# S5 scan mixed with a SiLU FFN: less loaded at the head, two rows spread by TensorE, B's copies earlier, last tile in two halves

## The chip, the core and the metric

The kernel runs on one core of a Trainium2 chip. The time is device microseconds of one execution; several runs are made and their median is compared. Lower is better. TensorE is called PE below, VectorE DVE, ScalarE ACT, GpSimd POOL and SyncE SP, as the profile calls them.

## The reference

Input x is 2048 time steps of 448 features in bf16. Two branches are computed from the same x and mixed by a gate of one number per time step.

```
g = sigmoid((x * gate_w).sum(-1))
# branch A: a diagonal complex state space model, P = 448 states
Lam_bar = exp(dt * Lam);   dt = exp(log_dt)
Bu[t]   = B_bar @ x[t];    B_bar = ((Lam_bar - 1) / Lam)[:, None] * B
h[t]    = Lam_bar * h[t-1] + Bu[t]          # 2048 steps
a[t]    = 2 * real(C @ h[t]) + x[t] * Dskip
# branch B: an FFN, 448 -> 1792 -> 448
b       = silu(x @ w1) @ w2
out     = g * a + (1 - g) * b
```

## The kernel before, in words

Time steps are taken in pairs: `x2` has 1024 rows of two steps (an even and an odd one, 896 numbers). A tile is 128 such rows of one parity, so there are 16 tiles; tile `2 * kt + odd` is parity `odd` of row block `kt`.

All work is written out by hand as one list per engine. `T.op(engine, thunk, reads, writes)` appends an instruction to an engine's list and puts waits before it, worked out from the names of the buffers; each engine then works through its list in order. So an instruction that waits holds up everything behind it in its list. `T.dma` does the same for a transfer on the queue of SP or ACT. The 8 banks of PSUM are handed out in turn by `nxt`, so a matmul also waits for whoever has to empty the bank it is given.

**Head.** The even half of the first 512 rows of x2 is loaded in its natural layout (`XH`, here inside the buffer of `CO`), transposed by PE, and copied by DVE into `XT`. The other transposed parts of x come by transposing DMAs (`ldt`, L225), as B's do (`BT`). SP's queue goes through: half of `XH`, parts of W1, parameter rows, W1's second half (`W1Ed`), two of B's transposes, x odd half 0 (`XTo0`, `XTr0`), B's remainders (`BT2`, `BT3`), `XTe1`, `XTo1`, `XTr1`, then two rows spread over 128 partitions (`GWB` from gate_w, `DB` from Dskip), then natural x (`XN0`, `XN1`), later `W2` and C. ACT's queue has the other half of `XH`, two rows, and W1's last 64 rows twice: into partitions 0 to 63 (`W1Ea`) and 64 to 127 (`W1Ez`). The contraction is 448 = 3 * 128 + 64; two remainders of 64 rows run side by side in the halves of the PE array, so x's remainder is needed in both halves too: `swap_xr` (L237) copies it across with DVE.

The four parameter rows (log_dt, Lambda_re, Lambda_im, Dskip) lie in `R`; `mm_cols` turns them into columns with PE (bank 7), DVE and ACT work out the coefficients in a chain of 128x4 operations (`dt`, `ph`, ..., `f2`, `afr`, `sn`, `cs`, `rr`; L446 to L473). From `f2` POOL makes phases (`phases(pt)`, L484 and L486, two operations of 128x1024 for each of 4 blocks), DVE takes off the whole turns (`phases2`, L491), and ACT makes tables of sine and cosine (`tables`, L496 to L501). The two buffers `G0` and `G1` alternate between the phase blocks. DVE also makes two copies of B's remainder, into the other partition half (L523) and, packed, into `BR` (L525).

**Middle.** `ffn1(c)` computes one of four column blocks c of silu(W1 x) (matmuls L330, remainders L343; ACT empties the banks, L371). The first 7 feature blocks of block 0 go another way, `ffn1_first` (L360). `ffn2(c, q)` multiplies by W2 (L663). `bu(pt, h)` makes B x for state block pt (L701, remainders L713), ACT evicts it into `VE` and `HS` (L723, L725, L730). The recurrence of a state block is a generator on DVE (`scan`, and `scan3` for the last 64 states): the even step is folded into the odd one, the result turned by the tables, run through a real scan (L771), turned back. `gate` (L596) is x * gate_w, which ACT adds up (`gate2`, L613) and `gate3` makes factors of; `skip` (L604) is x * Dskip in place. Both work on four blocks of four tiles. `ffn2(0, q)` is evicted by DVE (L671) and adds the skip product. The generators are started piece by piece from one list near the end of the program (L918 to L1002), which so sets the order of every engine.

**Tail.** Per tile, C times the states is added to what ACT seeded into the bank (`yseed`, L868): five matmuls on state parts that come early (`YA`, `yopen`), two on the parts that come late (`YB`, `yclose`; L876). `yout` evicts with the gate, by ACT (L897, first eight tiles) or DVE (L900, last eight), and stores the tile.

Of the kernel before, what the change touches and what calls it, by code (L numbers as in the profile page):

```python
# [19 lines left out]
D = 448  # L20
# [126 lines left out]
def gated_mix(nc, A_x, A_Lambda_re, A_Lambda_im, A_B_re, A_B_im, A_C_re, A_C_im, A_log_dt,  # L147
              A_Dskip, B_x, B_w1, B_w2, gate_w, out):
    with ExitStack() as ctx:
# [36 lines left out]
        R = sb("R", [4, 512], BF16)  # L186
# [22 lines left out]
        def xg(b):  # L209
            if b < 2:  # L210
                return CO[:, 4 * b:4 * b + 4, :], [f"CO{m}" for m in (range(4) if b == 0 else (1, 4, 5, 6))]
            if b == 2:
                return OT[:, 0:4, :], [f"OT{i}" for i in range(4)]
            v = TMPS[:, :, :].rearrange("p a b -> p (a b)").bitcast(BF16)
            return v[:, 0:4 * D].rearrange("p (k c) -> p k c", k=4), [f"TMP{i}" for i in range(3)]
# [34 lines left out]
        XH = CO[:, :, :].rearrange("p a b -> p (a b)")[:, 0:2048].rearrange("p (k c) -> p k c", k=4)  # L250
        COK = [f"CO{m}" for m in range(7)]
        x0 = x2[0:512, 0:512].rearrange("(k p) c -> p k c", p=128)
        for i, eng in enumerate(("sp", "act")):
            T.dma(eng, lambda e, i=i: e.dma_start(XH[:, 2 * i:2 * i + 2, :], x0[:, 2 * i:2 * i + 2, :]),
                  writes=COK[i:i + 1])
# [9 lines left out]
        ld("sp", W1E[:, 0:3, FA:], B_w1[0:384, FA:].rearrange("(j p) f -> p j f", p=128), "W1Ed")  # L265
        ld("act", W1E[0:64, 3, :], B_w1[384:448, :], "W1Ea")
        T.op("act", lambda e: e.activation(JK[:, 0:1], HP[:, :], AF.Exp), reads=["HP"], writes=["JK0"])
        ld("act", W1E[64:128, 3, :], B_w1[384:448, :], "W1Ez")
# [10 lines left out]
        def load_xn(h):  # L279
            ld("sp", XN[:, 8 * h * D:8 * (h + 1) * D].rearrange("p (k c) -> p k c", k=4),  # L280
               x2[h * 512:(h + 1) * 512, :].rearrange("(k p) c -> p k c", p=128), f"XN{h}")
# [6 lines left out]
        for dst, src, key in ((GWB, gate_w, "GW"), (DB, A_Dskip, "DB")):  # L288
            ld("sp", dst[:, :], row(src).partition_broadcast(128).rearrange("p o n -> p (o n)"), key)
# [25 lines left out]
        def ffn1_mm(c, fbs):  # L315

            odd, h = c // 2, c % 2
            hs = slice(h * 512, (h + 1) * 512)
            x0 = 4 * odd
            banks = [nxt() for _ in fbs]  # L320
            xk = XO[h] + [f"XR{h}b"] if odd else XE[h] + [f"XR{h}a"]

            rf = half[0]

            def mains():
                for fb, bank in zip(fbs, banks):
                    def mm(pe, fb=fb, bank=bank):
                        ins = None
                        for j in range(3):
                            ins = pe.matmul(ps[:, bank, :], W1E[:, j, fb * 128:(fb + 1) * 128],  # L330
                                            XT[:, x0 + j, hs], start=(j == 0 and not rf), stop=(j == 2 and rf))
                        return ins
                    wk = ["W1Ej0", "W1Ej1", "W1Ej2"] if fb < NFA else ["W1Ed"]
                    T.op("pe", mm, reads=wk + xk, writes=[f"ps{bank}"])

            def rests():
                def rest(pe):
                    ins = None
                    for i, (fb, bank) in enumerate(zip(fbs, banks)):
                        up = (i % 2 == 1) != bool(odd)  # L340
                        p = slice(64, 128) if up else slice(0, 64)
                        x = XT[p, x0 + 3, hs] if up == bool(odd) else XR[p, hs]
                        ins = pe.matmul(ps[:, bank, :], W1E[p, 3, fb * 128:(fb + 1) * 128], x,  # L343
                                        start=rf, stop=not rf)
                    return ins
                T.op("pe", rest, reads=["W1Ea", "W1Ez"] + xk, writes=[f"ps{bank}" for bank in banks])
            for part in (rests, mains) if rf else (mains, rests):
                part()
            half[0] = not rf
            return list(zip(fbs, banks))  # L350

        def ffn1_first():

            banks = [nxt() for _ in range(NFA)]
            for j in range(4):
                for fb, bank in enumerate(banks):
                    up = j == 3 and fb % 2 == 1
                    p = slice(64, 128) if up else slice(0, 128 if j < 3 else 64)
                    x = XR[p, 0:512] if up else XT[p, j, 0:512]
                    T.op("pe", lambda pe, fb=fb, bank=bank, j=j, p=p, x=x: pe.matmul(  # L360
                        ps[:, bank, :], W1E[p, j, fb * 128:(fb + 1) * 128], x, start=(j == 0), stop=(j == 3)),
                        reads=[f"W1Ej{j}" if j < 3 else "W1Ez" if up else "W1Ea", "XR0a" if up else f"XTe0{j}"],
                        writes=[f"ps{bank}"])
                if j == 0:
                    yield
            nxt()
            yield list(enumerate(banks))
# [20 lines left out]
        def rd():  # L388
            T.op("dve", lambda e: e.tensor_copy(R[:, D:512], R[:, 384:448]), reads=["R0", "R1", "R2", "R3"],
                 writes=["Rd"])  # L390
# [17 lines left out]
        for j in range(4):  # L408
            for i in range(2):
# [5 lines left out]
                T.op("pe", mm, reads=[COK[i], "ID"], writes=[f"ps{3 + j}"])  # L415
        for j in range(4):
# [4 lines left out]
        next(first)  # L421
        T.op("pe", mm_cols, reads=["R0", "R1", "R2", "R3", "Rd", "ID"], writes=["ps7"])
        first = next(first)
        T.op("dve", lambda e: e.tensor_copy(
            PV[:, :, :], ps[:, 7, 0:32].rearrange("p (t c) -> p t c", c=8)[:, :, 0:4]),
            reads=["ps7"], writes=["PV"])

# [30 lines left out]
        pact("mag", col("ar"), AF.Exp, ["ar"])  # L458
        T.op("act", lambda e: e.activation(JK[:, 0:1], HP[:, :], AF.Silu), reads=["HP"], writes=["JK0"])
# [12 lines left out]
        pact("cs", col("afr"), AF.Sin, ["afr", "HP"], scale=-SIN_SCALE, bias=HP[:, 0:1])  # L472
        ptt("rr", col("mag"), col("mag"), ALU.mult, ["mag"])  # L473

# [32 lines left out]
        def tmp(m):  # L507
# [4 lines left out]
        phases(0)  # L512
        phases(3)
        phases2(0)
        phases2(3)
# [5 lines left out]
        phases(1)  # L521
# [5 lines left out]
            BT[:, :, :].rearrange("p j (c n) -> p j c n", c=2)[:, :, :, 384:448]), reads=BTK, writes=["BR"])  # L527
        phases2(1)
        phases2(2)
        swap_xr("dve", 1, 0)  # L530
# [61 lines left out]
        def gate():  # L592
            for b in range(4):
                v = XN[:, 4 * b * D:4 * (b + 1) * D].rearrange("p (k c) -> p k c", k=4)
                o, ks = xg(b)
                T.op("dve", lambda e, v=v, o=o: e.tensor_tensor(  # L596
                    o, v, GWB[:, :].unsqueeze(1).to_broadcast([128, 4, D]), ALU.mult),
                    reads=[f"XN{b // 2}", "GW", f"XD{b}"], writes=ks)
                yield

        def skip():
            for b in range(4):
                v = XN[:, 4 * b * D:4 * (b + 1) * D].rearrange("p (k c) -> p k c", k=4)
                T.op("dve", lambda e, v=v: e.tensor_tensor(  # L604
                    v, v, DB[:, :].unsqueeze(1).to_broadcast([128, 4, D]), ALU.mult),
                    reads=[f"XN{b // 2}", "DB"], writes=[f"XD{b}"])
                yield

        def gate2():
            for t in range(2 * NKT):  # L610
                o, ks = xg(t // 4)
                v = o[:, t % 4, :]
                T.op("act", lambda e, t=t, v=v: e.activation(v, v, AF.Copy, accum_out=Z[:, t:t + 1]),  # L613
                     reads=ks, writes=[f"Z{t}"])
                if t % 8 == 7:
                    s = t // 8
# [3 lines left out]
                if t % 4 == 3:  # L620
# [24 lines left out]
        def ffn2_seed(q, off):  # L645
# [3 lines left out]
                 reads=[f"XD{tile // 4}", "GRO"], writes=[f"ps{bank}"])  # L649

        def ffn2(c, q):
# [18 lines left out]
            if c == 0:  # L670
                T.op("dve", lambda e: e.scalar_tensor_tensor(  # L671
                    bs(tile), ps[:, bank, 0:D], GT[:, 3, tile:tile + 1], xd(tile), ALU.mult, ALU.add),
                    reads=[f"ps{bank}", "GRI", f"XD{tile // 4}"], writes=ks)
# [191 lines left out]
        def yseed(kt, odd):  # L865
# [3 lines left out]
                 reads=[f"BS{tile}" if kt < 4 else f"XD{tile // 4}"], writes=[f"ps{bank}"])  # L869
            seeds.append((kt, odd, bank))  # L870

        def yhalf(ms, kt, odd, bank):
            def mm(pe):
                ins = None
                for m in ms:
                    ins = pe.matmul(ps[:, bank, 0:D], state(kt, odd, m), CO[:, m, :], start=False, stop=(m == YB[-1]),  # L876
# [12 lines left out]
        def yout(tile, bank):  # L889
            kt, odd = tile // 2, tile % 2  # L890
            i = n_o[0] % 8
            n_o[0] += 1
            o = OT[:, i, :] if i < 4 else xg(3)[0][:, i - 4, :]
# [5 lines left out]
            else:  # L899
                T.op("dve", lambda e: e.scalar_tensor_tensor(  # L900
                    o, ps[:, bank, 0:D], g, bs(tile), ALU.mult, ALU.add),
                    reads=[f"ps{bank}", "GT1_1", f"BS{tile}"], writes=[f"OT{i}"] + extra)
            outs.append(T.dma("sp", lambda e: e.dma_start(
                out2[kt * 128:(kt + 1) * 128, odd * D:(odd + 1) * D], o),
                reads=[f"OT{i}"], writes=[f"out{tile}"]))
# [14 lines left out]
        g1, g2, g3 = gate(), gate2(), gate3()  # L920
        t0, t1, t2, t3 = [tables(pt) for pt in range(4)]
        s0, s3, s1, s2 = scan(0), scan3(), scan(1), scan(2, True)
        g0 = skip()
# [4 lines left out]
        run(t0)  # L928
# [3 lines left out]
        bu(3, 0)  # L932
        f = ffn1(1)
# [5 lines left out]
        run(g1, 2)  # L939
# [41 lines left out]
        tiles = [(kt, odd) for kt in range(4) for odd in (1, 0)]  # L981
# [15 lines left out]
        opened = [yopen(), yopen()]  # L997
        while opened:
            ahead()
            yout(*yclose(*opened.pop(0)))  # L1000
            if seeds:
                opened.append(yopen())  # L1002
        T.wait_all("sp", outs)
# [35 lines left out]
```

## Time and profile before

| what | value |
|---|---|
| median of 7 runs | 143.45 us (142.76 to 144.05) |
| the profiled execution | 144.22 us, span 142.5 us |
| granted PE clock | 1.00 |
| busy, PE / DVE / ACT / POOL | 134.8 / 120.2 / 94.7 / 30.6 us |
| moved by DMA | 12.53 MB, 16228 of 23215 packets under 512 B |
| XN<-in_A_x_dram, issue to landing | 10.7 us (median of two) |
| W<-in_B_w_dram (W2), issue to landing | 15.8 us |

The span is from the first instruction to the last. In a row of the timeline the columns are start, duration, engine, line, operation, output and input with shapes and count; in brackets the engine's idle time before it and what ended that. In a row of the chain of waits: start, duration, what. In a row of the waits: who waited for whom, total, times, longest. In a row of the stretches: from and to, length, then busy time with count for PE, PE's weight loads, DVE, ACT and POOL, then the granted clock, the share of the DMA engines and GB/s.

### The profile page before, as it was taken

What the parts mean: (1) busy time and instruction counts of PE and PEld (TensorE: products, weight loads), DVE (VectorE), ACT (ScalarE), POOL (GpSimd) and SP (SyncE); (2) the same over time, 40 slices, a digit from 0 to 9 for tenths busy, and PEclk for the clock granted to TensorE, in tenths of its full rate; (3) what the DMA queues carried; (4) which work ended last, traced back from release to release, by engine and by line L of the source; (5) the groups of instructions that cost most, each with busy time, mean ns of one, the idle gap of its engine ahead of it and who ended that gap; (6) DMA issues with size and microseconds to landing.
All of it is one profiled execution on the core that took longest, in us unless ns stands there. A gap on an engine that the chain in (4) does not pass through costs nothing.

```text
span 142.5 us, 1870 instructions
## 1 busy us (share of the span) xinstructions
PE 134.8 (95%) x692; PEld 61.3 (43%) x699; DVE 120.2 (84%) x148; ACT 94.7 (66%) x155; POOL 30.6 (21%) x36
## 2 busy tenths in 40 slices
PE   6999997999989997999999999999999999999991
PEld 2443333334335542443455434435555555555550
DVE  1573779807999999999999999999999999999543
ACT  1359899679999955995999473877412536889000
POOL 7139999500000000059960000000000000000000
DMA  4999797999689400030020000000000000221222
GB/s 126 301 273 221 143 187 141 141 396 381 170 142 124 93 1 0 0 74 0 9 69 0 0 0 0 5 0 0 0 0 0 0 5 1 95 97 64 69 92 97
DMA packets 23215, 12.53 MB, mean 88 GB/s; under 512 B 16228, under 2 KB 22632, under 8 KB 23208
## 3 DMA queue, kind: packets, MB, share of 16 engines
q1 hardware_dynamic: 22548, 11.34, 33.9%
q10 hardware_dynamic: 660, 1.08, 2.6%
q8 instruction: 5, 0.08, 0.2%
q14 instruction: 2, 0.02, 0.0%
HBM read 6.26 MB, written 1.84 MB: 57 GB/s over the span
## 4 chain that ended last, share of the span: by engine, by line
PE 59%; SPq 15%; DVE 15%; DMA 7%; issue 2%; DVEq 1%
PE ps L663 22%; PE ps L876 15%; SPq L225 13%; PE ps L330 13%; DMA XN<-in_A_x_dram 7%; PE ps L701 6%; DVE G L771 3%; DVE Q L734 3%; PE ps L343 2%; SPq L222 2%; DVE IOTA L671 2%; DVE CO L596 2%; DVE XN L604 1%; PE ps L713 1%; DVE HS L737 1%
## 5 line engine op out<-in xcount | busy, mean ns | idle before, releaser
L663 PE MATMUL ps<-W,AT 128*128 128x448 bf16 x224 | 42.9, 352 | 0.6 <-DMA W<-in_B_w_dram 0.6
L330 PE MATMUL ps<-XT,W1E 128*128 128x512 bf16 x143 | 32.9, 379 | 1.4 <-issue 1.3
L371 ACT ACTIVATE AT<-ps 128x1024 bf16<-128x1024 f32 (+1 forms) x32 | 27.3, 917 | 6.6 <-PE ps L343 6.3
L663 PEld LDWEIGHTS ps<-W,AT 128*128 128x128 bf16 x224 | 21.8, 98 | 21.5 <-ACT SIN L496 1.1
L330 PEld LDWEIGHTS ps<-XT,W1E 128*128 128x128 bf16 x147 | 13.6, 97 | 20.0 <-issue 4.7
L701 PE MATMUL ps<-XT,BT 128*128 128x512 bf16 x70 | 16.1, 379 | 0.1
L676 ACT ACTIVATE BT<-ps,GT 128x448 bf16<-128x448 f32 x8 | 5.1, 634 | 13.1 <-PE ps L663 13.1
L551 POOL TENSOR_TENSOR P<-P 128x4 f32<-128x4 f32 x5 | 4.5, 895 | 35.0 <-DVE P L558 34.7
L876 PE MATMUL ps<-CO,HS 128*128 128x448 bf16 x56 | 11.6, 352 | 0.0
L876 PE MATMUL ps<-CO,VE 128*128 128x448 bf16 x56 | 11.6, 352 | 0.0
L723 ACT ACTIVATE VE<-ps 128x1024 bf16<-128x1024 f32 (+1 forms) x8 | 7.3, 916 | 6.1 <-PE ps L713 5.3
L771 DVE TENSOR_TENSOR_SCAN G<-P,Q 128x1024 f32<-128x1024 f32 (+1 forms) x6 | 11.3, 1920 | 0.0
L701 PEld LDWEIGHTS ps<-XT,BT 128*128 128x128 bf16 x72 | 6.8, 98 | 9.0 <-issue 1.3
L737 DVE SCALAR_TENSOR_TENSOR HS<-VE,P,G 128x512 bf16<-128x512 bf16 (+1 forms) x10 | 8.1, 856 | 0.2
L725 ACT ACTIVATE HS<-ps 128x1024 bf16<-128x1024 f32 (+1 forms) x8 | 7.3, 916 | 0.8 <-PE ps L701 0.8
L876 PEld LDWEIGHTS ps<-CO,VE 128*128 128x128 bf16 x56 | 5.5, 98 | 5.1
L876 PEld LDWEIGHTS ps<-CO,HS 128*128 128x128 bf16 x56 | 5.5, 98 | 5.1
L737 DVE SCALAR_TENSOR_TENSOR G<-VE,P,HS 128x1024 f32<-128x1024 bf16 (+1 forms) x5 | 7.5, 1493 | 0.2
L734 DVE TENSOR_TENSOR Q<-G,COS 128x2048 bf16<-128x2048 f32 (+1 forms) x4 | 7.0, 1755 | 0.1
L734 DVE TENSOR_TENSOR Q<-G,SIN 128x2048 bf16<-128x2048 f32 (+1 forms) x4 | 7.0, 1750 | 0.0
L343 PE MATMUL ps<-XT,W1E 64*128 64x512 bf16 x25 | 6.8, 379 | 0.0
L596 DVE TENSOR_TENSOR CO<-XN,GWB 128x1792 bf16<-128x1792 bf16 x2 | 2.2, 1092 | 5.2 <-DMA XN<-in_A_x_dram 5.2
(118 smaller groups left out, 196.8 us busy)
## 6 DMA issues: line engine op xcount, KB each, us to landing
XN<-in_A_x_dram SPq DMA_DIRECT2D x2, 896.0 KB, 10.7
W<-in_B_w_dram SPq DMA_DIRECT2D x1, 1568.0 KB, 15.8
out_dram<-OT SPq DMA_DIRECT2D x8, 112.0 KB, 1.7
out_dram<-TMPS SPq DMA_DIRECT2D x8, 112.0 KB, 1.7
W1E<-in_B_w_dram ACTq DMA_DIRECT2D x3, 224.0 KB, 6.0
W1E<-in_B_w_dram SPq DMA_DIRECT2D x1, 672.0 KB, 8.4
HS<-HS SPq DMA_DIRECT2D x4, 128.0 KB, 2.3
W1E<-in_B_w_dram SPq DMA_DIRECT2D x2, 224.0 KB, 4.7
```

The lines of the kernel that those rows point to most:

```text
L225: return T.dma("sp", lambda e: e.dma_start_transpose(dst, src), reads=reads, writes=[key, *also], group=group)
L330: ins = pe.matmul(ps[:, bank, :], W1E[:, j, fb * 128:(fb + 1) * 128], XT[:, x0 + j, hs], start=(j == 0 and not rf), stop=(j == 2 and rf))
L343: ins = pe.matmul(ps[:, bank, :], W1E[p, 3, fb * 128:(fb + 1) * 128], x, start=rf, stop=not rf)
L371: T.op("act", lambda e: e.activation(a[:, fb:fb + n, :], ps[:, bank:bank + n, :], AF.Silu), reads=[f"ps{bank + i}" for i in range(n)], wri ...
L663: ins = pe.matmul(ps[:, bank, 0:D], a[:, fb, q * 128:(q + 1) * 128], W2[:, fb, :], start=(first and fb == 0), stop=(fb == NFB - 1), skip_g ...
L701: ins = pe.matmul(ps[:, bank, :], bt(slice(0, 128), j, m), XT[:, 4 * odd + j, hs], start=(j == 0 and not rf), stop=(j == 2 and rf))
L723: T.op("act", lambda e: e.activation(VE[:, m0:m0 + n, hs], ps[:, be[0]:be[0] + n, :], AF.Copy), reads=pe_, writes=[f"V{m}_{h}" for m in ms])
L725: T.op("act", lambda e: e.activation(HS[:, m0:m0 + n, 8 + h * 512:8 + (h + 1) * 512], ps[:, bo[0]:bo[0] + n, :], AF.Copy), reads=po_, writ ...
L734: T.op("dve", lambda e: e.tensor_tensor(o, a, b, op), reads=reads, writes=writes)
L737: T.op("dve", lambda e: e.scalar_tensor_tensor(o, a, s, b, ALU.mult, ALU.add), reads=reads, writes=writes)
L771: T.op("dve", lambda e, c=c, init=init: e.tensor_tensor_scan(G[:, c, w], rb, Q1[:, c, w], init, ALU.mult, ALU.add), reads=[f"Q1{c}", "rr", ...
L876: ins = pe.matmul(ps[:, bank, 0:D], state(kt, odd, m), CO[:, m, :], start=False, stop=(m == YB[-1]), skip_group_check=True)
```

## The change

W1's last 64 rows are loaded once, in two parts by column, and DVE copies each part into partitions 64 to 127 (`double`). W1's second half is loaded in two parts. The rows gate_w and Dskip are no longer spread by DMA: PE multiplies a one-hot column, repeated 128 times, with `R` (`spread`, bank 7), and DVE copies the result out (`spread_out`); gate_w is a fifth row of `R`. The natural x of the first load goes to its place in `XN`, and `load_xn(0)` brings only the columns that are missing; the blocks of `gate` and `skip` for the first 8 tiles go by parity accordingly. On DVE the first gate block and the copies of B come before `phases2(3)`, `phases(1)` and `phases(2)` change places, and `swap_xr` comes before the last two `phases2`. Cosine table 0 comes after `bu(3, 0)`. At the tail three tiles are opened instead of two, the first eight tiles have another order, and the last tile is computed, evicted and stored in two halves of 224 columns.

```diff
-        R = sb("R", [4, 512], BF16)
+        R = sb("R", [5, 512], BF16)
...
-        XH = CO[:, :, :].rearrange("p a b -> p (a b)")[:, 0:2048].rearrange("p (k c) -> p k c", k=4)
-        COK = [f"CO{m}" for m in range(7)]
+        FB = FA + 512
+        XH = XN[:, 0:8 * D].rearrange("p (k c) -> p k c", k=4)
+        XA = ["XA0", "XA1"]
...
-        ld("sp", W1E[:, 0:3, FA:], B_w1[0:384, FA:].rearrange("(j p) f -> p j f", p=128), "W1Ed")
-        ld("act", W1E[0:64, 3, :], B_w1[384:448, :], "W1Ea")
+        for key, f0, f1 in (("W1Ed", FA, FB), ("W1Ee", FB, F_FF)):
+            ld("sp", W1E[:, 0:3, f0:f1], B_w1[0:384, f0:f1].rearrange("(j p) f -> p j f", p=128), key)
+        ld("act", W1E[0:64, 3, 0:FA], B_w1[384:448, 0:FA], "W1Ea0")
         T.op("act", lambda e: e.activation(JK[:, 0:1], HP[:, :], AF.Exp), reads=["HP"], writes=["JK0"])
-        ld("act", W1E[64:128, 3, :], B_w1[384:448, :], "W1Ez")
+        ld("act", W1E[0:64, 3, FA:], B_w1[384:448, FA:], "W1Ea1")
+        ld("act", R[4:5, 0:D], row(gate_w), "R4")
...
         def load_xn(h):
+            c0 = 0 if h else 512
...
-        for dst, src, key in ((GWB, gate_w, "GW"), (DB, A_Dskip, "DB")):
-            ld("sp", dst[:, :], row(src).partition_broadcast(128).rearrange("p o n -> p (o n)"), key)
         load_xn(0)
         load_xn(1)
...
+        def spread(i, c0):
+            T.op("pe", lambda pe: pe.matmul(ps[:, 7, c0:c0 + D], ID[0:i + 1, i:i + 1].to_broadcast([i + 1, 128]),
+                                            R[0:i + 1, 0:D], start=True, stop=True),
+                 reads=["R0", "R1", "R2", "R3", "ID"] + (["R4"] if i == 4 else []), writes=["ps7"])
+
         T.op("pe", mm_cols, reads=["R0", "R1", "R2", "R3", "Rd", "ID"], writes=["ps7"])
-        first = next(first)
+        spread(3, 64)
+        next(first)
...
+        def spread_out(dst, c0, key):
+            T.op("dve", lambda e: e.tensor_copy(dst[:, :], ps[:, 7, c0:c0 + D]), reads=["ps7"], writes=[key])
+
+        def double(i):
+            f = slice(i * FA, (i + 1) * FA)
+            T.op("dve", lambda e: e.tensor_copy(W1E[64:128, 3, f], W1E[0:64, 3, f]), reads=[f"W1Ea{i}"],
+                 writes=[f"W1Ez{i}"])
...
         pact("mag", col("ar"), AF.Exp, ["ar"])
+        spread_out(DB, 64, "DB")
+        spread(4, 0)
...
         pact("cs", col("afr"), AF.Sin, ["afr", "HP"], scale=-SIN_SCALE, bias=HP[:, 0:1])
+        double(0)
+        first = next(first)
         ptt("rr", col("mag"), col("mag"), ALU.mult, ["mag"])
+        spread_out(GWB, 0, "GW")
+        double(1)
...
-        phases(0)
-        phases(3)
-        phases2(0)
-        phases2(3)
         ptt("lr", col("mag"), col("cs"), ALU.mult, ["mag", "cs"])
...
-        phases(1)
+        phases(0)
+        phases(3)
+        phases2(0)
+        next(g1)
         phases(2)
         T.op("dve", lambda e: e.tensor_copy(BT[0:64, 3, :], BT[64:128, 3, :]), reads=BTK[2:4],
              writes=["BTz"] + BTK[2:4])
...
+        phases2(3)
+        phases(1)
+        swap_xr("dve", 1, 0)
+        phases2(2)
         phases2(1)
-        phases2(2)
-        swap_xr("dve", 1, 0)
...
-        run(t0)
+        run(t0, 2)
         bu(0, 0)
         load_w2()
         load_c()
         bu(3, 0)
+        run(t0)
...
-        run(g1, 2)
+        run(g1, 1)
         run(g0, 2)
...
-        tiles = [(kt, odd) for kt in range(4) for odd in (1, 0)]
+        tiles = [(0, 1), (1, 1), (0, 0), (2, 1), (1, 0), (3, 1), (2, 0), (3, 0)]
...
-        opened = [yopen(), yopen()]
+        opened = [yopen(), yopen(), yopen()]
+        kt, odd = tiles[-1]
         while opened:
             ahead()
             yout(*yclose(*opened.pop(0)))
-            if seeds:
+            if len(seeds) > 1 or tiles:
                 opened.append(yopen())
+        yseed(kt, odd)
+        for c in (slice(0, D // 2), slice(D // 2, D)):
+            kt, odd, bank = seeds.pop(0)
+            yhalf(YA + YB, kt, odd, bank, c)
+            yout(2 * kt + odd, bank, c)
```

## The prediction

> **What bounds the kernel now.** I read four views in this order: the page's busy row, the table of stretches (who is idle when), the chain of waits, then the timeline of the head and the tail.
>
> ```profile
> PE 134.8 (95%) x692; PEld 61.3 (43%) x699; DVE 120.2 (84%) x148; ACT 94.7 (66%) x155; POOL 30.6 (21%) x36
> ```
> ```profile
> 20.00:21.00 1.00, 0.77 (x6) 0.11 (x4) 0.93 (x2) 0.97 (x2) 0.92 (x2) 1.00 1.28 281
> 22.00:23.00 1.00, 0.78 (x3) 0.20 (x2) 1.00 (x2) 1.00 (x2) 0.92 (x2) 1.00 1.18 264
> 23.00:24.00 1.00, 0.33 (x2) 0.22 (x3) 0.83 (x3) 1.00 (x3) 0.76 (x3) 1.00 0.36 80
> 39.00:40.00 1.00, 0.57 (x3) 0.08 (x1) 1.00 (x3) 0.97 (x2) 0.00 (x0) 1.00 0.46 81
> 54.00:55.00 1.00, 0.24 (x4) 0.11 (x4) 1.00 (x3) 0.88 (x1) 0.00 (x0) 1.00 0.00 0
> 55.00:139.40 84.40, 84.00 (x437) 39.96 (x436) 79.82 (x81) 52.36 (x75) 11.15 (x9) 1.00 0.08 25
> ```
> The number after the length of a stretch is TensorE's (PE's) busy time. From 55 us to its last matmul PE is busy 84.00 of 84.40 us at granted clock 1.00, so that part only moves as a block. Whatever the change can give lies in PE's holes before 55 us: 1.17 us in 20 to 24 (0.23 + 0.05 + 0.22 + 0.67; the 0.05 is in 21:22), 0.62 us in 39 to 41, 0.76 us in 54 to 55. Together 2.55 us, 1.8% of the span.
>
> ```profile
> 23.28 9.79 DMA XN<-in_A_x_dram
> 33.06 0.02 issue
> 33.09 1.10 DVE CO L596
> ...
> 52.46 2.33 DVE IOTA L671 x4
> 54.79 0.05 issue
> 54.84 0.60 PE ps L713 x4
> ```
> ```profile
> DVE CO L596 <- DMA XN<-in_A_x_dram: 5.2, 1, 5.2
> PE ps L663 <- DMA W<-in_B_w_dram: 0.6, 1, 0.6
> ```
> The chain names the last hole: VectorE (DVE) stands idle 5.2 us for the natural x, then works without a pause to L671, which frees the banks PE needs at 54.84. The second wait is the hole at 40: W2, issued at 24.30, lands 15.8 us later. The holes of 20 to 24 are waits for DVE: L713 for the BR copy until 20.99, and the second FFN1 column block for `swap_xr`, which ends at 23.57 while PE starts at 23.67.
>
> ```profile
> 9.64 1.04 DVE L449 TENSOR_TENSOR P<-P 128x4 f32<-128x4 f32 x2
> 9.44 1.16 POOL L484 TENSOR_SCALAR FP<-IOTA,P 128x1024 f32<-128x1024 f32 x1 [5.25 <-DVE P L449]
> 19.32 0.62 DVE L523 COPY BT<-BT 64x896 bf16<-64x896 bf16 x1 [0.83 <-DMA BT<-in_A_B_im_dram]
> 139.03 1.27 DVE L900 SCALAR_TENSOR_TENSOR TMPS<-ps,GT,SIN 128x448 bf16<-128x448 f32 x2 [0.64 <-PE ps L876]
> ```
> The first two rows show a 128x4 operation that takes 0.16 us elsewhere held until GpSimd's (POOL's) instruction is over at 10.60. The last is the tail: two evictions of 0.68 us end at 140.30, 0.94 us after the last matmul (139.36).
>
> **The change, part by part.** The profiled execution took 144.22 us, span 142.5 and 1.72 around it; it is 0.77 above the median of 143.45. I make the sum on the span and subtract it from the median.
>
> *Transfers.* Gone: W1's second remainder (224 KB), GWB and DB (112 KB each), half of the first x block (512 KB); 960 KB. SP loses two issues (0.58 + 0.42 + 0.1 between them = 1.1 us) and gains one (W1Ee, about 0.43), which falls before the BT issue that sits 5.17 us in the queue anyway, so it costs nothing; without that cover it would be 0.43 us on every transpose. ACT's queue loses one W1 issue's bytes, and gains R4 (0.24 us) at 4 us, before its first wait at 4.7. 224 KB at some 300 GB/s bring the transposes 0.75 us forward, BT's landing from about 19.3 to 18.5; XN0 and W2 are issued 0.75 + 1.1 = 1.85 us earlier. In 28 to 36 us the engines move 380 to 410 GB/s, so 512 KB less before W2 are 1.3 us more. Estimate for W2: 37 to 38.8 instead of 40.1. XN0 (384 KB, first after the transposes) about 28.
>
> *VectorE's added work.* Two broadcast rows from PSUM (`spread_out`), between 0.42 (64x512 bf16 from PSUM, L418) and 0.68 each (128x448 f32 from PSUM, L671); I take 0.6. Two copies `double`: the nearest row is L523, same shape, 0.62 us, of which 0.38 overlap POOL's instruction that ends at 19.70; bare 0.24. The ends are 0.24 and 0.24 + 1.1 (one POOL instruction). The first `spread_out` lies in the serial chain ph to f2: POOL begins at about 10.05, not 9.44, and ACT's cosine comes at 11.3.
> Here a rule speaks against the change. The Trainium skill, "SBUF — State Buffer", section "Who interferes with whom", says that GpSimd and a VectorE copy in a two-port mode, or a VectorE operation with two SBUF inputs, hold a shared port pair exclusively, and the later one waits for the whole instruction. The rows above agree (0.62 for 0.24; 1.04 for two times 0.16). By the bare rows the four additions cost 1.7 us of VectorE; by the rule up to one POOL instruction (1.05 to 1.16) more at `double(0)`, `double(1)`, the gate product and the B copies. In the trace a second ready DVE instruction slips in before POOL's next one (`rr` directly after `afr`, 10.5 to 10.68), so I let `double(0)` run right behind `afr`: 11.3 to 11.55. PE's odd remainders waited for W1Ez until 11.11 and now wait until 11.55: **+0.45 us**, or +1.5 if the port is lost there. The two added matmuls on PE (0.2 each) vanish in that wait; alone they would be 0.4.
>
> *VectorE's order.* `double(1)`, lr, li, lis each can meet a POOL instruction; I put `phases2(0)` at 16.2 to 17.4 (before: 11.76). That is hidden: ACT reaches its sine table only at 18.43. Gate block 0 (1.09, L596) to 18.5, the B copies behind BT's landing and one POOL instruction to about 20, `phases2(3)` (1.22) to 21.2, `swap_xr` (0.29) to 21.5, 22.5 with another port loss. Behind it `phases2(2)` and, waiting for POOL's last operation, `phases2(1)` to about 26; the scan's first step starts there instead of 23.70, 2.4 us late. COS0 moves behind bu(3,0)'s evictions on ACT, whose 1.20 us wait at 25.8 takes it.
> PE: bu(0,0) and its remainder to 21.3 without a wait, bu(3,0) to 22.8, second FFN1 block from 22.8, not 23.67. So the 1.17 us are recovered and 0.3 to 0.45 given back at 11.5: **net -0.85**.
>
> *Middle.* PE reaches FFN2 at 39.58 - 0.85 = 38.7, with W2 there: **-0.62**. DVE from 26.1: scan step and scan3's step (4.2), gate 1 at about 30.4 (XN0 landed), skip 0 and 1 (2.1), 33.5; steps of 2.7 and 1.5, two gates (2.1), `turn` (8.2), gate3 (1.0) and three L671 (1.8) give 51 to 51.7 for the fourth, which was over at 54.79. PE wants the banks at 54.06 - 1.5 = 52.6: no hole, **-0.76**. That has about 1 us to spare. ACT, solid from 34 to 51.7, moves with PE at 31 (-0.85) and loses its 0.23 wait for CO, so the bank it frees last is there at 50.65, when PE wants it at 50.8; late next is therefore ACT, by 0 to 0.2 us.
>
> *Tail.* Fourteen half-width matmuls instead of seven: their weight loads take 0.098, a half of 448 columns takes about 0.094, so 1.45 us against 1.31, +0.14. Behind them DVE does three evictions of 0.68 and two of about 0.44; the last ends 0.73 after PE instead of 0.94: **-0.07**. A rule against it: the Trainium skill, "DMA: Bandwidth & Descriptors", "Specifications", has DMA line rate from 512 B and a read-modify-write below; the halves write 448 B rows. By the row (112 KB land in 1.7 us) a half is no slower and the sum stays at -0.07; if the rule costs the halved write what halving saves and another 0.3, +0.2. I take the row.
>
> Sum: -0.85 - 0.62 - 0.76 - 0.07 = -2.3; less 0.1 for ACT, **-2.2 us**: span 140.3, median **141.2 us**.
>
> **Rivals.**
> 1. *The port eats the head.* Every added copy loses against POOL: first remainders at 12.6 (+1.5), `swap_xr` at 23 to 23.6. Then 20 to 24 gives nothing; W2 and L671 still give 1.4: 142.1. For it: the two rows above. Against: POOL has only eight such operations and two of them must wait for VectorE.
> 2. *W2 does not come sooner.* Its end lies in 37 to 40, where only 80 to 90 GB/s flow; if what holds its last packets is not what was removed, PE waits until 40.1 again, and with it falls everything before. Left are L671's 0.76 and the tail, with ACT taking some: 142.7 to 143.4, say 143.0, no change to speak of. Against: 512 KB are missing from the full-rate stretch.
> 3. *Slower: VectorE is queued behind B.* The B copies now stand ahead of `phases2(3)`, `swap_xr`, the last phases and the scan. If BT lands at T, `swap_xr` ends between T + 2.0 (0.3 + 0.2 + 1.2 + 0.3) and T + 4.1 (two port losses). It decides when the FFN1 block starts past 23.67 + 0.62 + 0.76 + 0.07 + 0.72 = 25.8, that is T beyond about 22.8. At T = 23.5, block at 26.5: 143.45 + 2.83 - 1.45 = 144.8. For it: BT's issues are held 2.95 and 5.17 us, the queue is congested. Against: BT landed by 19.3 with more bytes ahead.
>
> **How the numbers follow.** About 0.5% (0.7 us) is what a measurement of this kernel tells from no change. Main case 0.60 (141.2; its own range 140.2 to 142.2), rival 1 0.15 (142.1), rival 2 0.12 (143.0), rival 3 and other losses 0.13 (144.8). Faster: 0.60 + 0.15 = 0.75; same 0.12; slower 0.13. The range runs from 139.9 (all holes, 2.55 us; 0.3 at the tail; 0.7 for scatter, as the lowest single run lies 0.7 below the median) to 143.8, past rival 2's end by the same scatter on its upper side; rival 3 is left out.
>
> **What would show it.** Right: no DVE wait on XN of several us; PE idle in 20 to 24 under 0.4; FFN2 starting below 39; no L713 wait on L671; `double(0)` just behind `afr`. Wrong: `double(0)` over 1 us, or PE's first remainders after 12; W2 landing at 40; a new PE wait for `swap_xr` or ACT's L371; a hole in PE after 55 where VectorE's last scan is late.

## The result, and the profile after

| what | before | after |
|---|---|---|
| median of all runs shown | 143.45 us (31 runs, 142.67 to 144.37) | 141.74 us (12 runs, 141.39 to 142.78) |
| the profiled execution, and its span | 144.22 us, 142.5 us | 141.74 us, 140.0 us |
| granted PE clock | 1.00 | 1.00 |
| W2, issue to landing | 15.8 us | 10.5 us |
| moved by DMA | 12.53 MB | 11.54 MB |

The ratio after to before is 0.989, with a 95% interval of 0.9868 to 0.9912: the interval lies clear of 1, so it is faster, by 1.7 us in the medians. The two profiled executions lie 2.5 us apart; the difference between 1.7 and 2.5 is taken up below. Against the prediction of 141.2 us the kernel is 0.5 us slower, inside the range.

The page of after, its busy row, and then the first row of its part on the chain that ended last (shares of the span by engine):

```profile
PE 134.9 (96%) x701; PEld 62.8 (45%) x708; DVE 124.8 (89%) x153; ACT 94.8 (68%) x156; POOL 30.0 (21%) x36
...
PE 92%; DVE 4%; issue 1%; DVEq 0%; ACT 0%
```

PE works as long as before (134.8 us then), DVE 4.6 us longer, and the chain now is PE almost from end to end. The stretches of after (PE's busy time stands behind the length):

```profile
11.00:12.00 1.00, 0.65 (x4) 0.21 (x5) 0.94 (x3) 0.59 (x2) 0.92 (x2) 1.00 1.28 287
12.00:13.00 1.00, 0.84 (x7) 0.31 (x5) 1.00 (x2) 0.92 (x3) 0.83 (x2) 1.00 0.92 175
20.00:21.00 1.00, 1.00 (x7) 0.34 (x7) 1.00 (x2) 0.97 (x2) 0.63 (x1) 1.00 0.89 121
22.00:23.00 1.00, 0.95 (x6) 0.42 (x5) 0.97 (x2) 1.00 (x2) 0.94 (x1) 1.00 1.09 213
23.00:24.00 1.00, 1.00 (x6) 0.46 (x5) 1.00 (x1) 1.00 (x3) 0.92 (x2) 1.00 0.59 124
39.00:40.00 1.00, 1.00 (x7) 0.49 (x5) 1.00 (x2) 0.97 (x2) 0.00 (x0) 1.00 0.11 22
54.00:55.00 1.00, 1.00 (x6) 0.49 (x5) 0.97 (x2) 1.00 (x2) 0.00 (x0) 1.00 0.00 0
55.00:137.20 82.20, 81.80 (x433) 39.67 (x433) 76.16 (x78) 51.50 (x74) 11.27 (x9) 1.00 0.08 25
```

All three holes are closed: in 20 to 24, at 39 and at 54 PE is busy, up to 0.05 us. Of PE's idle time behind 10 us and ahead of the block from 55 on, what is left stands in 11 to 13 (0.35 + 0.16 us); the 0.35 are a wait for the copy of W1's last remainder rows. The timeline of after, DVE's rows of that place, and POOL's first two operations:

```profile
10.41 0.96 DVE L464 TENSOR_TENSOR P<-P 128x4 f32<-128x4 f32 x1
11.41 0.39 DVE L440 COPY W1E<-W1E 64x896 bf16<-64x896 bf16 x1
11.82 0.89 DVE L464 TENSOR_TENSOR P<-P 128x4 f32<-128x4 f32 x1
```
```profile
10.21 1.16 POOL L505 TENSOR_SCALAR FP<-IOTA,P 128x1024 f32<-128x1024 f32 x1 [6.02 <-DVE P L464]
11.45 1.26 POOL L507 TENSOR_SCALAR G<-FP 128x1024 f32<-128x1024 f32 x1
```

`afr` at 10.41, a 0.16 us operation, is held until POOL's operation is over at 11.37. `double(0)` (L440) starts just before POOL's next one and takes 0.39 us, and the operation behind it is held again, to 12.71. PE takes the odd remainders up at 11.85.

The chain of after in the middle, and the last evictions from its timeline:

```profile
38.87 5.30 PE ps L697 x28
44.20 5.47 PE ps L697 x28
49.72 2.54 PE ps L735 x11
52.26 0.97 PE ps L747 x8
```
```profile
136.30 1.39 DVE L934 SCALAR_TENSOR_TENSOR TMPS<-ps,GT,SIN 128x448 bf16<-128x448 f32 x3
```

L697 (L663 before), L735 (L701) and L747 (L713) follow each other without a wait for W2 or for DVE. The last eviction ends at 137.69, 0.53 us after PE's last matmul at 137.16; before it was 0.94.

### The profile page after: what moved, and what is told of

It is laid out like the page before. It is cut to its first block, busy times and chain, and to the rows that moved or that the text cites. A ratio compares the mean times of both kernels' runs of the same rounds, so it can differ in the third digit from the quotient of the medians.

```text
span 140.0 us, 1895 instructions
## 1 busy us (share of the span) xinstructions
PE 134.9 (96%) x701; PEld 62.8 (45%) x708; DVE 124.8 (89%) x153; ACT 94.8 (68%) x156; POOL 30.0 (21%) x36
## 2 busy tenths in 40 slices
DMA packets 23473, 11.54 MB, mean 82 GB/s; under 512 B 16485, under 2 KB 23018, under 8 KB 23466
## 4 chain that ended last, share of the span: by engine, by line
PE 92%; DVE 4%; issue 1%; DVEq 0%; ACT 0%
PE ps L697 30%; PE ps L331 23%; PE ps L910 14%; PE ps L735 13%; PE ps L344 4%; PE ps L747 2%; PE ps L403 2%; PE ps L361 2%; DVE P L464 1%; PE ps L414 1%; DVE TMPS L934 1%; DVE P L461 1%; DVE DB L436 0%; DVE W1E L440 0%; DVEq L1046 0%
## 5 line engine op out<-in xcount | busy, mean ns | idle before, releaser
L697 PE MATMUL ps<-W,AT 128*128 128x448 bf16 x224 | 43.0, 353 | 0.0
L697 PEld LDWEIGHTS ps<-W,AT 128*128 128x128 bf16 x224 | 21.8, 98 | 20.9 <-ACT AT L372 0.5
L372 ACT ACTIVATE AT<-ps 128x1024 bf16<-128x1024 f32 (+1 forms) x32 | 27.3, 916 | 5.5 <-PE ps L344 5.1
L735 PE MATMUL ps<-XT,BT 128*128 128x512 bf16 x70 | 16.1, 380 | 0.1
L600 POOL TENSOR_TENSOR P<-P 128x4 f32<-128x4 f32 x5 | 5.6, 1121 | 28.2 <-DVE P L607 27.9
L910 PE MATMUL ps<-CO,VE 128*128 128x448 bf16 (+1 forms) x63 | 11.6, 332 | 0.0
L910 PE MATMUL ps<-CO,HS 128*128 128x448 bf16 x56 | 11.6, 353 | 0.0
L805 DVE TENSOR_TENSOR_SCAN G<-P,Q 128x1024 f32<-128x1024 f32 (+1 forms) x6 | 11.3, 1918 | 0.0
L735 PEld LDWEIGHTS ps<-XT,BT 128*128 128x128 bf16 x72 | 6.8, 97 | 9.0 <-issue 1.3
L910 PEld LDWEIGHTS ps<-CO,VE 128*128 128x128 bf16 x63 | 6.1, 98 | 4.7
L910 PEld LDWEIGHTS ps<-CO,HS 128*128 128x128 bf16 x56 | 5.5, 98 | 5.1
L934 DVE SCALAR_TENSOR_TENSOR OT<-ps,GT,BT 128x448 bf16<-128x448 f32 x4 | 2.7, 684 | 4.4 <-PE ps L910 4.4
## 6 DMA issues: line engine op xcount, KB each, us to landing
W<-in_B_w_dram SPq DMA_DIRECT2D x1, 1568.0 KB, 10.5
```

The source lines that it names most:

```text
L372: T.op("act", lambda e: e.activation(a[:, fb:fb + n, :], ps[:, bank:bank + n, :], AF.Silu), reads=[f"ps{bank + i}" for i in range(n)], wri ...
L600: T.op("pool", lambda e: e.tensor_tensor(col(o), a, b, op), reads=ra, writes=[o])
L697: ins = pe.matmul(ps[:, bank, 0:D], a[:, fb, q * 128:(q + 1) * 128], W2[:, fb, :], start=(first and fb == 0), stop=(fb == NFB - 1), skip_g ...
L735: ins = pe.matmul(ps[:, bank, :], bt(slice(0, 128), j, m), XT[:, 4 * odd + j, hs], start=(j == 0 and not rf), stop=(j == 2 and rf))
L805: T.op("dve", lambda e, c=c, init=init: e.tensor_tensor_scan(G[:, c, w], rb, Q1[:, c, w], init, ALU.mult, ALU.add), reads=[f"Q1{c}", "rr", ...
L910: ins = pe.matmul(ps[:, bank, c], state(kt, odd, m), CO[:, m, c], start=False, stop=(m == YB[-1]), skip_group_check=True)
```

## The experiments

All ratios are to the kernel before, run beside it on the same chip. Diffs are against the kernel before where the label begins with b, against the one after where it begins with a.

**b_again: the kernel before, unchanged, profiled once more.** No edit.

> The kernel before, unchanged, profiled once more. The profiled pair moved by 2.5 us, the medians by 1.7. Theory: the profile of before was one of its slow executions, with a larger hole in PE behind W2 or behind VectorE's wait for x than a usual one has; then this profile has a span of 141.4 to 142.0 and its holes before 55 us add up to about 1.8 us, not 2.55. Rival: the holes are the same in every execution and the extra time lies elsewhere (outside the span or after 55 us); then the holes are again 2.5 us.

It took 143.19 us, span 141.5, and lies 0.3 us below the median of 143.45; the first profile (144.22) lies 0.8 above. Its row of the waits, then two rows of its timeline, where the odd remainders begin and where the third hole was:

```profile
DVE CO L596 <- DMA XN<-in_A_x_dram: 3.1, 1, 3.1
```
```profile
11.53 0.39 PE L360 MATMUL ps<-XR,W1E 64*128 64x512 bf16 x1 [0.46 <-DMA W1E<-in_B_w_dram]
...
53.40 1.04 PE L713 MATMUL ps<-XT,BT 64*128 64x512 bf16 x8
```

DVE waits 3.1 us for the natural x and not 5.2, because XN lands 9.8 us after its issue and not 10.7, and the eight L713 matmuls run in one piece. The hole of 0.76 us does not exist in this execution, and the wait for W2 is 0.4 us, not 0.6. So the third term of the sum belongs to the execution that was profiled first. The odd remainders of the first block wait for their load until 11.53, where the first profile had 11.11. PE's idle time in 20 to 24 is there in both (0.24 and 0.79 us in 22 to 24 here).

**b_tail: the tail alone, on the kernel before.**

```diff
-        def yhalf(ms, kt, odd, bank):
+        def yhalf(ms, kt, odd, bank, c=slice(0, D)):
...
-        tiles = [(kt, odd) for kt in range(4) for odd in (1, 0)]
+        tiles = [(0, 1), (1, 1), (0, 0), (2, 1), (1, 0), (3, 1), (2, 0), (3, 0)]
...
-        opened = [yopen(), yopen()]
+        opened = [yopen(), yopen(), yopen()]
...
+        for c in (slice(0, D // 2), slice(D // 2, D)):
+            yhalf(YA + YB, kt, odd, bank, c)
+            yout(2 * kt + odd, bank, c)
```

> Before with the tail alone changed (order of the first eight tiles, three tiles opened, the last one in halves). My sum had -0.07 us for it; in the two profiles the stretch from the last matmul to the last eviction shrank by 0.4 us (0.94 to 0.53) with PE's own end moved by no more than its start. Theory of the sum: no difference that can be told, ratio 0.998 to 1.001. Rival: the tail is worth 0.3 to 0.4 us, ratio 0.997. If rows of 448 B are costly on the way out, ratio above 1.001.

143.13 us, ratio 0.9972 (0.9943 to 1.0001), which is 0.4 us, with an interval that just touches none. The profile is clearer than the ratio. PE ends at 138.64, and the last evictions are these:

```profile
137.77 1.39 DVE L900 SCALAR_TENSOR_TENSOR TMPS<-ps,GT,SIN 128x448 bf16<-128x448 f32 x3
```

They end at 139.16, 0.52 us behind PE instead of 0.94. From there to the end of the span it is 2.3 us, in both profiles of before 2.2, so the write of rows of 448 bytes costs about 0.1 us if anything, and about 0.3 of DVE's 0.4 us reach the span. This profile has the old head and middle, and no hole at L713 either: two of three profiled executions of that part are without it, and this one (143.22) lies at the median of its kernel. Its head is later than in the other two: B lands at 20.25, and the second FFN1 block starts at 24.42 instead of 23.67. W2 lands 13.8 us after its issue, at 39.7, and is not waited for; PE then waits for ACT's banks instead, and FFN2 takes 10.97 us, as after, and not 10.75.

**a_order: the kernel after, with DVE's old order.** `phases2(3)` ahead of B's copies, `swap_xr` last, the first gate block back in the middle; the less loaded head, the copies and the tail stay.

```diff
+        phases(0)
+        phases(3)
+        phases2(0)
+        phases2(3)
         ptt("lr", col("mag"), col("cs"), ALU.mult, ["mag", "cs"])
...
-        phases(0)
-        phases(3)
-        phases2(0)
-        next(g1)
+        phases(1)
...
-        phases2(3)
-        phases(1)
-        swap_xr("dve", 1, 0)
-        phases2(2)
         phases2(1)
+        phases2(2)
+        swap_xr("dve", 1, 0)
...
-        run(g1, 1)
+        run(g1, 2)
```

> After, with VectorE's order of before in the head (both first phases2, then the lr group, B's copies late, swap_xr last, gate block 0 at its old place). Theory: B's copies early are worth the 1.0 us that PE idles in 20 to 25 us in the kernel before and 0.05 after; PE again waits for BR or swap_xr, 0.7 to 1.1 us, and since W2 has been there since 33 us nothing behind it takes that up: 142.4 to 142.8, ratio 0.993 to 0.996. Rival: the order costs nothing because PE is held by the landing of B or by ACT in the head; 141.7 to 142.0.

144.0 us, ratio 1.0039 (1.0011 to 1.0067): slower than before. Against after that is 1.0039 / 0.989 = 1.015, 2.1 us, more than the whole gain. Its timeline, `swap_xr` on DVE and what waited for it on PE:

```profile
25.26 0.29 DVE L237 COPY XR<-XT 64x512 bf16<-64x512 bf16 x1
25.65 2.75 PE L331 MATMUL ps<-XT,W1E 128*128 128x512 bf16 x12 [1.55 <-issue]
```

The same copy in after's timeline:

```profile
21.93 0.29 DVE L237 COPY XR<-XT 64x512 bf16<-64x512 bf16 x1
```

`swap_xr` comes 3.3 us later than in after and 2.0 us later than in before (23.28). In this execution about 1.0 us of that is a late head (DVE reads the parameter columns at 8.77 instead of 7.80), and it is the slowest of its twelve runs; the medians' 2.1 us are the better size. What is left fits DVE's new work ahead of it (two `spread_out` of 0.62 and two `double` of 0.39 and 0.96, 2.6 us, part of which falls into time in which DVE was idle in before). So the change without its order is a loss of half a microsecond. PE starts 0.1 us after `swap_xr` ends, though the profile names no releaser for its wait of 1.55 us. The new order on the kernel before, without the added work, was not run; what it is worth there is open.

**a_load512: the kernel after, with 512 KB loaded again between XN0 and XN1,** into a buffer that nothing reads before it is overwritten.

```diff
+        ld("sp", AT[1][:, 10:14, :], x2[0:512, 0:512].rearrange("(k p) c -> p k c", p=128), "AT1x")
```

> After, with 512 KB of x loaded once more, between XN0 and XN1, into space that is not used until later (the value is never read). If the missing bytes are what brought W2 in time, W2 lands 1.3 us later, at 37 to 39, XN1 1.3 us later, and PE waits at FFN2 by 0 to 0.6 us: 141.7 to 142.3. Rival: the bytes are hidden and the earlier issue alone did it; no difference in time, W2 lands before PE asks.

141.86 us, ratio 0.9896 (0.9861 to 0.993): no difference from after. W2 is issued 1.1 us later (23.85) and lands at 35.2, not 33.3, more than 3 us before PE asks (38.8). Of its time from issue to landing (11.3 us for 10.5) nothing can be laid to the load, since a_again below has 11.5 without it.

**b_load512: the same 512 KB in the kernel before,** ahead of XN0, with the same line.

> Before, with the same 512 KB load placed ahead of natural x (XN0) in SP's queue. Theory: before stands at an edge: VectorE's wait for XN0 (3.1 us in one profile, 5.2 in the other) opens a hole in PE at 54 us only beyond about 4 us, and W2 is just late; 1.3 us more give the hole of 1 to 1.5 us in nearly every execution and 0.6 to 1.3 us at FFN2: 145.0 to 146.2, ratio 1.011 to 1.019. After took the same load without a change. Rival: transfers are hidden in before too; ratio under 1.005.

144.88 us, ratio 1.0118 (1.0094 to 1.0142): 1.7 us slower. Two rows of PE's timeline:

```profile
41.22 10.75 PE L664 MATMUL ps<-W,AT 128*128 128x448 bf16 x56 [1.22 <-DMA W<-in_B_w_dram]
...
55.55 0.60 PE L714 MATMUL ps<-XT,BT 64*128 64x512 bf16 x4 [0.45 <-DVE IOTA L672]
```

Both holes of the first profile are back, W2's at twice the size; W2 lands at 41.1 instead of 40.1. The same bytes cost nothing in one kernel and 1.7 us in the other: before stands at the edge where the loads come just in time, and after has some 5 us to spare (W2 landed at 33.3, PE asks at 38.7).

**a_rows_dma: the kernel after, with gate_w and Dskip spread by DMA again,** no `spread`, no `spread_out`.

```diff
-        ld("act", R[4:5, 0:D], row(gate_w), "R4")
...
+        for dst, src, key in ((GWB, gate_w, "GW"), (DB, A_Dskip, "DB")):
+            ld("sp", dst[:, :], row(src).partition_broadcast(128).rearrange("p o n -> p (o n)"), key)
...
-        spread(3, 64)
...
-        spread_out(DB, 64, "DB")
-        spread(4, 0)
...
-        spread_out(GWB, 0, "GW")
...
-        next(g1)
...
-        run(g1, 1)
+        run(g1, 2)
```

> After, with the rows of gate_w and Dskip spread over the partitions by DMA again, in their old place in SP's queue, PE's two spreads and VectorE's two copies out left out, and gate block 0 back in its old place, since its row now lands late. W2 landed at 33.3 us in the profile of after, 40.1 before; the 512 KB load showed that bytes alone move it by about 1 us. If the spread rows are what held the engines, W2 lands at 38 or later and PE has a hole before FFN2: 142.2 or more. Rival: only the two issues in SP's queue count; everything behind them is 1.1 us later, W2 lands by 35.5, and PE, which has neither the spreads nor their wait, gains 0.2 to 0.4 in the head: 141.3 to 141.7.

141.55 us, ratio 0.9885 (0.9854 to 0.9916): the same as after. The two issue rows, first of this kernel, then of after (size, and us to landing):

```profile
W<-in_B_w_dram SPq DMA_DIRECT2D x1, 1568.0 KB, 13.3
```
```profile
W<-in_B_w_dram SPq DMA_DIRECT2D x1, 1568.0 KB, 10.5
```

W2 is issued at 24.36 and not 22.75, and lands at 37.7 and not 33.3. Two rows of 112 KB make it 4.4 us later than in that profile of after; a_again's landed at 34.7, so 3.0 later than there. But PE asks for it at 38.66 and finds it there. The landing came close to the expectation's theory (38 or later), the time to its rival (141.3 to 141.7). So to spread the two rows by PE buys an earlier W2, with 4 to 5 us to spare instead of 1.0, and no time.

**a_double_early: `double(0)` moved ahead of `f2`,** so that POOL has not begun.

```diff
+        double(0)
...
-        double(0)
```

> After, with the first copy of W1's remainder moved in VectorE's list from behind afr to before f2, before GpSimd starts. Theory: in the profile of after the copy ends at 11.80 because afr is held by GpSimd until 11.37; moved ahead it ends by 9.9, PE's hole of 0.5 to 0.7 us at 11 to 13 goes and everything behind moves: 141.1 to 141.3, ratio to before 0.984 to 0.986. GpSimd starts 0.3 us later. Rival: ACT's eviction of the first banks (cosine first, at 11.4) or VectorE's later order becomes the bound and PE waits there instead: no gain.

142.0 us, ratio 0.9905 (0.9877 to 0.9934): no faster than after. `double(0)` runs at 9.23 and the odd remainders at 10.81, a microsecond sooner. The timeline of this kernel, what follows on ACT and PE:

```profile
11.52 0.30 ACT L467 ACTIVATE P<-P,HP 128x4 f32<-128x4 f32 x1 [1.49 <-DVE P L464]
...
12.66 2.53 PE L331 MATMUL ps<-XT,W1E 128*128 128x512 bf16 x11 [0.82 <-ACT AT L372]
```

PE now waits 0.82 us for ACT to empty its first bank. ACT's eviction stands behind the cosine, the cosine behind `afr`, and `afr` behind POOL. Two waits lay on top of each other, and only one was taken away: 0.17 us at the next group (12.66 for 12.83).

**a_afr_early: `nfr` and `afr` moved ahead of `f2` too.**

```diff
+        pts("nfr", col("fr"), -1.0, None, ALU.mult, ALU.bypass, ["fr"])
+        ptt("afr", col("fr"), col("nfr"), ALU.max, ["fr", "nfr"])
+        double(0)
...
-        pts("nfr", col("fr"), -1.0, None, ALU.mult, ALU.bypass, ["fr"])
-        ptt("afr", col("fr"), col("nfr"), ALU.max, ["fr", "nfr"])
...
-        double(0)
```

> After, with nfr, afr and the first copy of W1's remainder ahead of f2, so that VectorE has made them before GpSimd starts. With the copy alone moved, PE waited 0.8 us for ACT's first eviction instead, which stands behind the cosine, and that behind afr, held by GpSimd until 11.5. Theory: now the cosine is done by 10.5, the first bank is empty by 11.8, PE goes on at about 12.0 instead of 12.83, and 0.7 us of it reach FFN2 (38.0): 141.0 to 141.3. Rival: BT's landing and the B copies, or ACT solid from 16 us on, take it back before FFN2: 141.6 to 141.8.

141.51 us, ratio 0.9897 (0.9866 to 0.9927). Both waits are gone in its timeline: the next group of FFN1 begins at 12.23, not 12.83, FFN2 at 38.32, not 38.71, and the span is 139.6, not 140.0. The ratio does not tell it from after. The profile is 0.4 us shorter, and a_again's below is 0.2 longer, so what is left to win at this place is small.

**a_double_dma: W1's second remainder by DMA again,** no `double`, the rest of after kept.

```diff
+        ld("act", W1E[64:128, 3, 0:FA], B_w1[384:448, 0:FA], "W1Ez0")
...
+        ld("act", W1E[64:128, 3, FA:], B_w1[384:448, FA:], "W1Ez1")
...
-        double(0)
...
-        double(1)
```

> After, with W1's second remainder loaded by DMA again (224 KB more in ACT's queue) and VectorE's two copies left out. Theory: PE's first remainders no longer wait for VectorE behind the shared port, but the cosine behind afr still holds ACT's first eviction until 11.8, so PE gains 0.1 to 0.2 us there; BT lands 0.5 to 0.8 us later, which VectorE, at the B copies from 18.5 on, passes on in part: within 0.3 us of after, ratio to it 0.998 to 1.003. Rival: the bytes at the head are what pays; B's copies and swap_xr come 0.8 us later and PE with them: 142.4.

145.74 us, ratio 1.0105 (1.0071 to 1.014). Neither theory foresaw this. The two loads stand ahead of gate_w's row (`R4`) in ACT's queue, and PE's `spread` of it stands ahead of the remainders. A row of the waits, then the stretches (the granted clock is the third number from the end):

```profile
PE ps L426 <- DMA R<-in_gate_w_dram: 2.7, 1, 2.7
```
```profile
13.00:14.00 1.00, 0.41 (x3) 0.20 (x5) 0.01 (x1) 0.00 (x0) 0.92 (x2) 1.00 1.29 208
14.00:15.00 1.00, 1.00 (x7) 0.24 (x3) 0.98 (x3) 0.69 (x2) 0.90 (x2) 0.64 1.18 241
15.00:16.00 1.00, 1.00 (x3) 0.28 (x3) 0.99 (x2) 1.00 (x3) 1.00 (x1) 0.50 1.08 227
16.00:17.00 1.00, 1.00 (x3) 0.30 (x2) 1.00 (x2) 1.00 (x3) 0.12 (x1) 0.50 0.93 201
17.00:18.00 1.00, 1.00 (x4) 0.40 (x3) 1.00 (x2) 0.84 (x2) 0.59 (x1) 0.65 0.55 104
```

PE stands still for 2.7 us and then runs at half speed for some three; FFN2 starts at 42.59, in a_again on the same chip at 38.93. B lands later too, at 20.73 for a_again's 19.23. Its copies on DVE, at a time when POOL has nothing to do (20.38 to 22.83):

```profile
20.73 0.39 DVE L570 COPY BT<-BT 64x896 bf16<-64x896 bf16 x1 [2.47 <-DMA BT<-in_A_B_im_dram]
21.25 0.29 DVE L572 COPY BR<-BT 128x512 bf16<-128x512 bf16 x1
```

In after, with POOL at work, the same two took 1.12 and 1.00 us (18.53 and 19.77). What the 224 KB alone are worth is not shown by this run, since a row of 0.9 KB was late because of its place in a queue; the variant with `R4` ahead of these loads wasn't run.

**a_again: the kernel after, once more,** as a control beside the next one.

> After, unchanged, run once more beside the next two so that they are compared on the same chip: ratio to before 0.987 to 0.991 and a span of 139.7 to 140.4, with PE's hole of about 0.5 us in 11 to 13 us.

142.05 us, ratio 0.9853 (0.9819 to 0.9887); FFN2 begins at 38.93, the span is 140.2.

**a_afr_rows: a_afr_early with the rows by DMA,** the edits of a_afr_early and a_rows_dma together.

> The two that helped in their profiles put together: afr and the first copy ahead of f2, and the two rows by DMA as in the kernel before, without spreads on PE and copies out on VectorE. PE has no hole in 10 to 15 us and 0.5 us less work in the head: FFN2 could start at 37.8 instead of 38.7. W2 landed at 37.7 with the rows by DMA, so it is about there: 140.8 to 141.2, ratio to after 0.994 to 0.997. Rival: W2 or XTe1 (VectorE waited 1.0 us for it before swap_xr) now binds and nothing is left of it: 141.5 to 141.8.

141.54 us, ratio 0.9811 (0.9774 to 0.9849). Beside the control on the same chip it is 0.9811 / 0.9853 = 0.996, and the intervals overlap, so no gain is shown. Its profiled execution was its slowest run: PE waited 1.2 us for x's second even half, which in after it doesn't. None of the versions run here is shown to beat the kernel after.

## Why the prediction was right, and what it had wrong

The sum, step by step: times of the same place in the first profile of before, in b_again and in after. The last two columns are after's difference to each.

| PE, or as named | before | b_again | after | predicted | to before | to b_again |
|---|---|---|---|---|---|---|
| second FFN1 block starts | 23.67 | 23.79 | 22.97 | -0.85 | -0.70 | -0.82 |
| FFN2 starts | 40.20 | 40.12 | 38.71 | -1.47 | -1.49 | -1.41 |
| bu behind it (L701) starts | 51.00 | 50.93 | 49.72 | -1.4 | -1.28 | -1.21 |
| next FFN1 block starts | 57.98 | 56.97 | 55.76 | -2.1 | -2.22 | -1.21 |
| PE's last matmul ends | 139.36 | 138.35 | 137.16 | -2.0 | -2.20 | -1.19 |
| DVE's last eviction ends | 140.30 | 139.29 | 137.69 | -2.2 | -2.61 | -1.60 |

(Predicted: -0.85, -0.62, ACT's 0.1 lost, -0.76, the tail's +0.14 on PE and -0.07 with DVE, summed as they fall.)

- **The holes of 20 to 24: right.** `swap_xr` was put at 21.2 to 21.5 and ran at 21.93 to 22.22, the FFN1 block at 22.8 and started at 22.97. The way there had two errors of opposite sign. The port held more than was taken: `double(1)`, `rr`, lr, lis, both B copies each took 0.9 to 1.1 us. And `double(0)` slipped in behind `afr` as said, but `afr` itself ended at 11.37 and so the odd remainders ran at 11.85, +0.74 for the +0.45 (+0.32 to b_again, where they waited for their load). Rival 1's mechanism was there with half of its price at the remainders. The rows agree with the shared port of the Trainium skill's "SBUF — State Buffer", "Who interferes with whom": in a_double_dma the B copies took 0.39 and 0.29 us without POOL, in after 1.12 and 1.00 with it. So the bare price of `double` was 0.39, not 0.24, and the wait belongs in the sum at nearly every DVE copy that meets POOL.
- **W2: right in time, wrong in size.** The wait of 0.62 is gone. The landing, put at 37 to 38.8, was 33.3. Of that, a_rows_dma gives 3.0 to 4.4 us to the two spread rows, for which the sum had counted SP's 1.1 us of issues alone; of the 4.4, the issue is 1.6. With the rows by DMA the landing was 37.7, inside the estimate. Rival 2 needed it to stay at 40. How the gain divides between this step and the one before depends on the execution: in b_tail the second FFN1 block starts at 24.42 and W2 is not waited for, yet FFN2 starts at 40.16, as in the other two. The two steps together are 1.4 to 1.5 us.
- **L671's hole, -0.76: the step that failed is "I make the sum on the span and subtract it from the median".** The profiled execution was 0.77 us above the median, and the hole of 0.76 belonged to it. b_again and b_tail have none, and b_tail's profile lies at its median. Taken off the median, this time was subtracted from executions most of which, as far as three profiles show, don't have it. b_load512 shows the mechanism itself: delay the loads, and the hole is there (0.45). So the mechanism was right and the term mis-sized: 0.76 was put down, about 0 was there to win.
- **ACT, 0 to 0.2 us late next: right in size, at another bank.** FFN2 takes 10.96 us for 10.75, its weight loads waiting 0.5 us for ACT's L372, and 0.21 us are lost between the second and the third row of the table. The bank in question is free at 44.14, and the weight loads for it wait from 43.73 on. The bank that the prediction named came at 50.67, for 50.65, and held up weight loads alone.
- **The tail: mis-sized, -0.07 for -0.4.** The two halves were to cost PE 0.14 us. PE's part from L910 on (L876 before) took as long as before (139.36 - 118.18 = 21.18; 137.16 - 115.97 = 21.19), so no cost of the added weight loads shows; and DVE ended 0.53 behind PE, not 0.73. About 0.3 of the 0.4 reach the span. The rule on DMA rows under 512 B, weighed there, shows about 0.1 us in b_tail if anything.
- **Rival 3, slower by DVE's queue: not in this order, but near.** B's copies ran at 18.53 and 19.77, on time. a_order shows what the rival was about from the other side: the same added DVE work with the old order made the kernel slower than before by 0.4%, since `swap_xr` then stands behind it. The prediction treated the order as one gain among several; with the added work in place it is worth 2.1 us, more than the whole.

The two size errors (0.76 too much, some 0.3 too little at the tail) nearly explain the miss: 141.2 + 0.76 - 0.3 = 141.7, against 141.74 measured. They have opposite signs, so that the prediction came within 0.5 us is in part luck. From b_again the three terms are 0.82 in the head, 0.4 by W2 less ACT's bank, and 0.3 at the tail, 1.5 us, as the two spans say (141.5 and 140.0), beside the medians' 1.7.

What stays open: the price of W1's 224 KB alone; what the new order is worth without the added work; what makes XN land late in some executions of before and not in others; and whether moving `afr` ahead of POOL is a real gain of some 0.3%.

## What to carry to other kernels

A hole in the profile that ends at a transfer is worth no more than its share in the usual execution: put the profile's own time beside the median first, and look at a second profile of the same kernel before its holes are summed. Work moved from DMA to an engine has to be placed: with the same additions, the order of one engine's list decided here between 1.7 us faster and half a microsecond slower. And where two waits end close together (W1's rows and ACT's bank at 11 to 12.7 us), taking one away shows the other; both have to go.

## What the runs showed of the hardware that was not expected

- In a_double_dma a pause of PE cost twice. PE was idle for 2.7 us, and the granted clock then was 0.50 from 15 to 17 us, with 0.64 and 0.65 in the stretches beside; twelve FFN1 matmuls took 3.91 us there, 2.75 elsewhere. The Trainium skill, "TensorE: Matmul & The Clock Gate", Part 1, has the half clock follow an idle window of about 3.4 us, free-running; here a shorter pause was enough. All six runs of that kernel have a mean granted clock of 0.988, all others here 0.996 or more. After a_order's pause of 1.55 us the stretches stayed at 1.00. That the pause is what set off the half clock is read from their order in time; no run changed the pause alone.
- Two rows of 112 KB, spread over 128 partitions by DMA, delayed a transfer queued behind them by 4.4 us (a_rows_dma, 37.7 for 33.3), 1.6 us of it in SP's issues and 2.8 in the transfer; beside a_again (landed at 34.7) it is 3.0, of which 1.8 in the transfer. The whole kernel moves only 0.23 MB more (11.77 for 11.54).
- In after DVE got in between two POOL operations with an instruction that stood ready: the gap is under 0.1 us, and `double(0)` ran in 0.39 us there, while the next in line was held for 0.89.
